# A fused attention and expert kernel: rows turned one slot sooner, and two tiles whose second layer keeps h stationary

## The chip, the cores and the metric
The kernel runs on one core of a Trainium2 chip. Its time is the device time of one launch in microseconds (us). Before the change the median of three runs is 2148.25 us (2147.32 to 2149.73).

## What is computed
The reference first computes an attention without softmax over 8 batches of 2496 tokens, and then sends each token through one of 8 experts, a layer of 1024 and a layer back to 256, by the largest logit.
```python
scores = z @ z.T / S
x = u * (np.maximum(scores, 0) ** 2 @ v)          # 8 x 2496 rows of 256
logits = x @ w_gate + modality_bias[modality_id]
e = argmax(logits); gate = softmax(logits)[e]
out[token] = gate * (np.maximum(x @ w1[e], 0) @ w2[e])
```

## The kernel before, in words
**Precision.** A value that enters a product is split into a high part, rounded by ScalarE, and a low part, the remainder that VectorE takes; a product is three products (high x high, high x low, low x high).

**The attention part** runs to about 1249 us in the profile. As it goes, each token's row is scattered by GpSimd (`scatter`, L718 to L720) to its expert's stretch of a DRAM table `xs`. Nothing that the change touches lies there.

**The expert part** takes tiles of 512 rows of one expert (`run_tile`, called by the loop near the program's end). The tiles are t = -4 to 34: four early ones of the fullest expert (EARLY = 4), whose rows are complete before the rest is routed, and 35 whole ones (UNC = 35). After tile 34's first half stands a quarter tile (`quarter_tile`, 128 rows, lines L1496 to L1521), woven into tile 34. What may remain is handled by branches at the end (L1656), which this input skips. For tile t:

- `fetch` (L875, L877) brings rows out of `xs` into `xg`, one or two tiles ahead. `turn_blocks` (VectorE, `xt`, L941), `part_high` (ScalarE, `xh`, L948) and `part_low` (VectorE, `xl`, L953) turn them and split them. They run inside the tile before, at the slot that `turn_at` gives for the transposition and one slot later for the split.
- The first layer, `up`, makes for f = 0 to 7 six products of 512 columns into `ph` (L1365); ScalarE takes `hh` from it (L1369), VectorE `hl` (L1370). f runs in two groups of four.
- The second layer follows each group. In a **staged** tile, `down` holds w2 stationary and streams h: per group sixteen products with hh and then eight with hl, of 512 columns (L1439), into two banks `po`. The result stands turned, with features on partitions. So `send` transposes it on VectorE (`squared`, L1451), stores it in a DRAM buffer `stage` by four transfers (L1455), and leaves the rest for the next tile: at its slot 2 one load `back` (L1464), at slots 4, 5, 6, 6 a scaling by the gate on ScalarE (L1469) and the put of 128 rows by GpSimd (L1389).
- In a tile that is **not staged**, `down_high` and `down_low` hold h stationary: per group sixteen products of 512 columns (L1376, both halves of w2 side by side) and sixteen of 256 columns (L1380), into four banks. Rows stand on partitions at once, and `finish` puts them out at the tile's end: per 128 rows two scalings `part` on ScalarE (L1420) and two sums `y` on VectorE (L1421), in turn, and a put on GpSimd (L1389).
- Inside a tile, `aside(f)` is called at slots f = 0 to 9. Slot 5 comes after `up` of f = 5; slot 6 after that of f = 7, ahead of the second layer; slot 7 within or after the second layer. It emits what was put off, then a quarter of the next tile's weight split (`part_weights_high`, ScalarE, L918; `part_weights_low`, VectorE, L922) at slots 2 to 5, and then the turning.

**Order.** Every engine works its instructions in the order in which this code emits them (the schedule is manual). SP carries the loads and stores, GpSimd the row transfers.

**The puts.** A tile's first put waits until the four of the tile before have landed, since two tiles of an expert may share rows. Tile 34 and the quarter tile are **kept**: their rows are put after the skipped branches, the quarter tile's first, and the others after it has landed. On the skipped path GpSimd's queue waits until earlier row transfers have landed before it goes on.

Before the change all tiles but 34 are staged:
```python
def is_staged(t):
    return t < UNC - 1
def turn_at(t):
    return {-EARLY: 3, 1 - EARLY: 3, UNC - 1: 2}.get(t, KF - 2)
```

Of the kernel before, what the change touches and what calls it, by code (L numbers as in the profile page):

```python
# [9 lines left out]
F32 = mybir.dt.float32  # L10
# [6 lines left out]
P = 128  # L17
# [10 lines left out]
def tile_attention_moe(ctx: ExitStack, tc: tile.TileContext, ut, v, zt, mid, wg, mb, w1, w2, out):  # L28
# [12 lines left out]
    B, S, D = v.shape  # L41
# [4 lines left out]
    KD, KF = D // P, F // P  # L46
    J = T // P
# [8 lines left out]
    EARLY = min(4, (B - 1) * S // E // T)  # L56
    UNC = -(-N // T) - EARLY
# [796 lines left out]
        ready["n"] = len(scatters)  # L854

    def is_staged(t):
        return t < UNC - 1

    def fetch(t, r0=0, nj=J):

        n = t + EARLY
        cell = first[0:1, 1:2] if t < 0 else meta[0:1, t, 0:1]
        row = nc.sync.value_load(cell, min_val=0, max_val=(E - 1) * CAP if t < 0 else E * CAP - T)
        k = fetched["n"] % 2
        fetched["n"] += 1
        nt = nj * P
        xg = head[k].tile([P, T // BLK, KD * BLK], F32, tag=f"xg{k}", name="xg")[:, 0:nt // BLK, :]
        side = small.tile([P, J, 2], F32, tag="gate", bufs=4, name="gate")[:, 0:nj, :]
        r0 += n * T if t < 0 else 0
        src = xs[bass.ds(row + r0 if r0 else row, nt), :]  # L870
        dmas = []
        for b in range(P // BLK):
            cols = slice(b * KD * BLK, (b + 1) * KD * BLK)
            rows_of = src[:, cols].rearrange("(t i) c -> i t c", i=BLK)
            dmas.append(nc.sync.dma_start(out=xg[b * BLK:(b + 1) * BLK], in_=rows_of))  # L875
        order = "(p j) c -> p j c" if is_staged(t) else "(j p) c -> p j c"
        dmas.append(nc.sync.dma_start(out=side, in_=src[:, D:XW].rearrange(order, j=nj)))  # L877
        wait_rows([ins_of(i) for i in dmas])
        TL[t] = (side, xg)
# [315 lines left out]
    with tc.manual_schedule(engines={ET.PE, ET.Activation, ET.DVE, ET.Pool, ET.SP}):  # L1195
# [33 lines left out]
        def ready_at(p):  # L1229
            t = 0.0  # L1230
            for d, lag in p.after:
                if d.start is None:
                    return None
                t = max(t, d.end + lag)
            return t
# [14 lines left out]
        while left:  # L1250
# [6 lines left out]
            for p in lists[e][:80]:  # L1257
                t = ready_at(p)
# [89 lines left out]
    mp = ph2.enter_context(tc.tile_pool(name="mp", bufs=2, reuse_waits="tile"))  # L1348
# [37 lines left out]
    def put_rows(ids, j, y, group):  # L1386

        i = ins_of(
            nc.gpsimd.indirect_dma_start(  # L1389
                out=out,  # L1390
                out_offset=bass.IndirectOffsetOnAxis(ap=ids[:, j:j + 1], axis=0),
                in_=y,
                in_offset=None,
                bounds_check=N - 1,
                oob_is_err=False,
            )
        )
        tc.declare_no_dep(i, group=group, reason="a tile's tokens are distinct")
        tc.add_to_no_dep_group(group, i)
        for s in done:  # L1400
            tc.add_manual_dep(i, s.name, data, reason="rows that two tiles of an expert share")
        return i

    def finish(t, po, group, kept=None):

        side, TL[t] = TL[t][0], None
        tag = "ids" if kept is None else "kept_ids"
        ids = mp.tile([P, J], I32, tag=tag, bufs=4 if kept is None else 2, name="ids")[:, 0:len(po)]
        nc.vector.tensor_copy(out=ids, in_=side[:, :, 1])
        mine = []  # L1410
        for j in range(len(po)):
            gate = side[:, j, 0:1]
            part2 = mp.tile([P, D], F32, tag="part2", bufs=2, name="part2")
            keep = kept is not None
            y = mp.tile([P, D], F32, tag="kept" if keep else "y", bufs=J + 1 if keep else 2, name="y")
            of_y = y.rearrange("p (b k c) -> p k b c", k=KD, c=BLK)
            for k in range(KD):
                cols = slice(k * P, (k + 1) * P)
                high, low = po[j][:, cols], part2[:, cols]
                nc.scalar.mul(out=low, in_=po[j][:, D + k * P:D + (k + 1) * P], mul=gate)  # L1420
                nc.vector.scalar_tensor_tensor(  # L1421
                    out=of_y[:, k], in0=high.rearrange("p (b c) -> p b c", c=BLK), scalar=gate,
                    in1=low.rearrange("p (b c) -> p b c", c=BLK), op0=ALU.mult, op1=ALU.add,
                )
            if keep:
                kept.append((ids, j, y, group))
            else:
                mine.append(put_rows(ids, j, y, group))
            if j == len(po) - 1 and not kept:
                done[:] = mine  # L1430
                written.extend(mine)
            yield
# [91 lines left out]
        yield from finish(t, [po], f"out{t}{part}", kept)  # L1524

    def turn_at(t):
        return {-EARLY: 3, 1 - EARLY: 3, UNC - 1: 2}.get(t, KF - 2)

    def run_tile(t, ahead, extra={}, part="", beside=iter(()), kept=None):
        if len(TL[t]) < 3:  # L1530
            turn(t)
        staged = is_staged(t) and not part
        po = [ps_o.tile([P, 2 * D], F32, tag="o", name="po") for _ in range(KD if staged else TL[t][0].shape[1])]
        h = {}
# [96 lines left out]
    kept = []  # L1631
# [89 lines left out]
```

## Time and profile before
| | us |
|---|---|
| median of three runs | 2148.25 |
| the profiled execution | 2147.46 |
| its span in the profile | 2145.7 |
| TensorE busy | 2115.1 (99%) |
| VectorE busy | 1617.1 (75%) |
| ScalarE busy | 1443.2 (67%) |
| GpSimd busy | 404.4 (19%) |

The span runs from the first to the last instruction; the execution's own time has 1.8 us more around it. The granted clock of TensorE is 0.996 of full speed over the span, so its time is 2.4 GHz time nearly throughout. Busy times of the engines overlap. The ends of products are modelled, so their starts are what is compared below. In time-line rows the brackets at the end tell how long the engine idled before the instruction and what released it; PEld is the weight load that runs beside the products.

### The profile page before, as it was taken

The numbers are of one execution on the slowest core, as the hardware profiler recorded it, in microseconds if no ns is written. First come the engines' busy times: TensorE is split into PE (matmuls) and PEld (weight loads), VectorE is DVE, ScalarE is ACT, GpSimd is POOL, SyncE is SP. The second block draws the span as 40 slices with busy tenths as digits, with TensorE's granted clock in tenths as the row PEclk, the third lists the DMA queues.
The fourth block names the chain that finished last, engine by engine and source line by source line (L and its number), as shares of the span: only waits on it lengthen the run. The fifth ranks groups of instructions, "written<-read, shape, count | busy, mean of one in ns | idle before, by whom it ended". The sixth has DMA issues, their size and how long they took to land.

```text
span 2145.7 us, 44124 instructions
## 1 busy us (share of the span) xinstructions
PE 2115.1 (99%) x16582; PEld 1842.8 (86%) x16582; DVE 1617.1 (75%) x2363; ACT 1443.2 (67%) x2214; POOL 404.4 (19%) x342
## 2 busy tenths in 40 slices
PE   9999999999999999999999999999999999999995
PEld 7888999888888899999999987888888888888884
DVE  8888889888889799799799765666566666656663
ACT  8778788788788788688788753454444545444453
POOL 0000210310300301301302304122222212212121
PEclk9999999999999999999999999999999999999998
DMA  7987877877976966967967826676766767676661
GB/s 193 281 238 168 254 202 180 255 202 181 274 186 164 300 176 163 300 174 183 288 160 181 255 61 191 176 207 177 192 192 186 205 175 207 179 189 196 185 196 48
DMA packets 630122, 424.83 MB, mean 198 GB/s; under 512 B 216170, under 2 KB 579690, under 8 KB 629898
## 3 DMA queue, kind: packets, MB, share of 16 engines
q1 hardware_dynamic: 614810, 380.72, 66.7%
q0 software_dynamic: 15088, 41.21, 5.4%
q8 instruction: 131, 2.15, 0.4%
q14 instruction: 93, 0.76, 0.1%
HBM read 263.66 MB, written 158.13 MB: 197 GB/s over the span
## 4 chain that ended last, share of the span: by engine, by line
PE 75%; DVE 11%; ACT 5%; DMA 4%; issue 3%; SPq 1%; POOL 0%; ACTq 0%; POOLq 0%; DVEq 0%
PE acc L492 44%; PE ph L1365 13%; PE po L1439 10%; PE s L343 6%; DVE hl L1370 3%; DVE w L922 3%; DVE xl L953 2%; DMA out_dram<-back,ids 2%; DVE xt L941 2%; ACT xh L948 2%; ACT w L918 2%; PE po L596 2%; DMA squares<-turn 1%; SPq L416 1%; ACT back L1469 1%
## 5 line engine op out<-in xcount | busy, mean ns | idle before, releaser
L492 PE MATMUL acc<-ah,vh 64*128 64x512 f32 (+1 forms) x3120 | 460.2, 384 | 0.9 <-DVE ah L439 0.5
L492 PE MATMUL acc<-al,vh 64*128 64x512 f32 (+1 forms) x3120 | 449.5, 382 | 0.1
L466 DVE TENSOR_TENSOR al<-r,ah 128x1024 fp32r<-128x1024 f32 (+4 forms) x514 | 431.6, 873 | 23.7 <-ACT ah L456 21.6
L492 PE MATMUL acc<-ah,vl 64*128 64x512 f32 (+1 forms) x3120 | 448.4, 382 | 0.0
L1369 ACT ACTIVATE hh<-ph 128x512 fp32r<-128x512 f32 x312 | 182.9, 600 | 369.1 <-PE ph L1365 369.1
L720 POOL DMA_INDIRECT xs<-x,sloti x160 | 195.2, 1220 | 1097.8 <-ACT ah L456 385.4
L1365 PE MATMUL ph<-xh,w 128*128 128x512 f32 x1248 | 399.0, 390 | 0.3 <-ACT xh L948 0.3
L1370 DVE SCALAR_TENSOR_TENSOR hl<-ph,hh 128x512 fp32r<-128x512 f32 x312 | 211.5, 688 | 249.0 <-ACT hh L1369 248.9
L456 ACT CAST ah<-r 128x1024 fp32r<-128x1024 f32 (+5 forms) x475 | 333.8, 746 | 38.5 <-PE acc L492 24.0
L492 PEld LDWEIGHTS acc<-al,vh 64*128 64x128 f32 x3120 | 332.6, 184 | 26.9 <-DVE al L466 0.8
L492 PEld LDWEIGHTS acc<-ah,vh 64*128 64x128 f32 x3120 | 327.3, 184 | 27.1 <-DVE ah L439 0.9
L492 PEld LDWEIGHTS acc<-ah,vl 64*128 64x128 f32 x3120 | 327.0, 184 | 26.4
L1389 POOL DMA_INDIRECT out_dram<-back,ids x152 | 199.8, 1314 | 623.0 <-ACT w L918 557.0
L1439 PE MATMUL po<-hh,w 128*128 128x512 f32 x1216 | 288.6, 389 | 1.1 <-ACT hh L1369 1.1
L1365 PEld LDWEIGHTS ph<-xh,w 128*128 128x128 f32 x1248 | 234.3, 188 | 49.0 <-ACT xh L948 0.7
L1439 PEld LDWEIGHTS po<-hh,w 128*128 128x128 f32 x1216 | 228.1, 188 | 49.2 <-ACT hh L1369 2.0
L356 ACT ACTIVATE r<-s 128x1024 f32<-128x1024 f32 (+2 forms) x206 | 209.3, 1017 | 84.3 <-PE s L343 67.3
L1365 PE MATMUL ph<-xl,w 128*128 128x512 f32 x624 | 246.9, 396 | 2.9 <-DVE xl L953 0.8
L398 DVE STREAM_TRANSPOSE turn<-r 128x1024 f32<-128x1024 f32 x158 | 195.6, 1238 | 33.6 <-ACT r L432 24.1
L432 ACT ACTIVATE r<-r 128x1024 f32<-128x1024 f32 (+2 forms) x205 | 215.7, 1053 | 5.4
L343 PE MATMUL s<-zm 64*128 64x512 f32 (+3 forms) x1452 | 203.8, 377 | 1.7 <-ACT r L356 1.5
L922 DVE TENSOR_TENSOR w<-wq,w 128x1024 fp32r<-128x1024 f32 x148 | 178.2, 1223 | 33.0 <-ACT w L918 32.9
(173 smaller groups left out, 1988.1 us busy)
## 6 DMA issues: line engine op xcount, KB each, us to landing
squares<-turn SPq DMA_DIRECT2D x632, 128.0 KB, 2.9
r<-squares SPq DMA_DIRECT2D x158, 512.0 KB, 5.6
wq<-in_moe_w_dram SPq DMA_DIRECT2D x148, 512.0 KB, 5.7
ut<-in_ut_dram SPq DMA_DIRECT2D x40, 512.0 KB, 3.8
xg<-xs SPq DMA_DIRECT2D x156, 128.0 KB, 3.7
stage<-squared SPq DMA_DIRECT2D x152, 128.0 KB, 2.9
back<-stage SPq DMA_DIRECT2D x38, 512.0 KB, 3.7
vr<-in_v_dram SPq DMA_DIRECT2D x32, 512.0 KB, 7.3
```

The lines of the kernel that those rows point to most:

```text
L343: nc.tensor.matmul(out=s[t][:, w], lhsT=lhs, rhs=mv[halves[t], ql, w], start=n == 0, stop=n == 2)
L356: nc.scalar.activation(out=r[:, t, w], in_=s[t][:, w] if g < 2 else s[:, :, w], func=AF.Relu, scale=INV)
L398: nc.vector.transpose(out=turned_to, in_=x)
L432: nc.scalar.square(out=a[:, t, w], in_=r[:, t, w])
L456: copy(out=y, in_=x)
L466: nc.vector.tensor_tensor(out=y, in0=x, in1=h.bitcast(F32), op=ALU.subtract)
L492: nc.tensor.matmul(out=acc[b, c][r][dh][:, :w], lhsT=V[b, k // J][y][halves[r], k % J, dh * P:(dh + 1) * P], rhs=x[halves[r], t, :w], star ...
L922: nc.vector.tensor_tensor(out=lo, in0=x, in1=hi.bitcast(F32), op=ALU.subtract)
L1365: nc.tensor.matmul(out=ph, lhsT=lhs, rhs=rhs[:, k, :], start=n == 0, stop=n == 3 * KD - 1)
L1370: nc.vector.scalar_tensor_tensor(out=hl, in0=ph, scalar=0.0, in1=hh.bitcast(F32), op0=ALU.max, op1=ALU.subtract)
L1389: nc.gpsimd.indirect_dma_start(out=out, out_offset=bass.IndirectOffsetOnAxis(ap=ids[:, j:j + 1], axis=0), in_=y, in_offset=None, bounds_ch ...
L1439: nc.tensor.matmul(out=po[k], lhsT=w[:, f, q, k * P:(k + 1) * P], rhs=h[f][part], start=f == q == part == 0, stop=f == KF - 1 and part == 1,)
```

## The change
Three lines change.
```diff
@@ -854,7 +854,7 @@
         ready["n"] = len(scatters)
 
     def is_staged(t):
-        return t < UNC - 1
+        return t < UNC - 2 and t != 2 - EARLY
 
     def fetch(t, r0=0, nj=J):
 
@@ -1412,7 +1412,7 @@
             gate = side[:, j, 0:1]
             part2 = mp.tile([P, D], F32, tag="part2", bufs=2, name="part2")
             keep = kept is not None
-            y = mp.tile([P, D], F32, tag="kept" if keep else "y", bufs=J + 1 if keep else 2, name="y")
+            y = mp.tile([P, D], F32, tag="kept" if keep else "y", bufs=J + 1 if keep else J, name="y")
             of_y = y.rearrange("p (b k c) -> p k b c", k=KD, c=BLK)
             for k in range(KD):
                 cols = slice(k * P, (k + 1) * P)
@@ -1524,7 +1524,7 @@
         yield from finish(t, [po], f"out{t}{part}", kept)
 
     def turn_at(t):
-        return {-EARLY: 3, 1 - EARLY: 3, UNC - 1: 2}.get(t, KF - 2)
+        return {-EARLY: 3, 1 - EARLY: 3, UNC - 1: 2}.get(t, KF - 3 if is_staged(t) else KF - 2)
 
     def run_tile(t, ahead, extra={}, part="", beside=iter(()), kept=None):
         if len(TL[t]) < 3:
```
`is_staged` now leaves out t = 33 (UNC - 2) and t = -2 (2 - EARLY) besides t = 34: these two run `down_high`, `down_low` and `finish`. `y` gets four buffers, one for each put of a tile. `turn_at` gives slot 5 in place of 6 for the staged tiles from -1 to 32; tiles -2 and 33 keep slot 6, and -4, -3 and 34 keep theirs.

VectorE's order in one staged tile of the many, from its last weight remainder on (`w`), with hl of f = 6 and 7, the next tile's `xt` and `xl`, and its own `squared`:
```order
 L1370 SCALAR_TENSOR_TENSOR hl<-ph,hh 128x512
 L922 TENSOR_TENSOR w_1_20158<-wq,w_1_20158 128x4x256
-L1370 SCALAR_TENSOR_TENSOR hl<-ph,hh 128x512 x2
-L941 STREAM_TRANSPOSE xt<-xg 128x1024
+L941 STREAM_TRANSPOSE xt<-xg 128x1024
+L1370 SCALAR_TENSOR_TENSOR hl<-ph,hh 128x512 x2
 L953 TENSOR_TENSOR xl<-xt,xh 128x1024
 L1451 STREAM_TRANSPOSE squared<-po 128x16x32 x2
```

The transposition stands ahead of the last two hl; the remainder `xl` keeps its place behind them. On ScalarE the order of a staged tile is the same as before.

ScalarE from the end of tile -2 (its `xh` for tile -1) to `xh` for tile 0, before:
```order
L948 CAST xh<-xt 128x1024
L1369 ACTIVATE hh<-ph 128x512 x4
L918 CAST w_1_20157<-wq 128x1024 x2
L1369 ACTIVATE hh<-ph 128x512
L1469 ACTIVATE back<-back,gate 128x256
L918 CAST w_1_20158<-wq 128x4x256
L1369 ACTIVATE hh<-ph 128x512
L1469 ACTIVATE back<-back,gate 128x256
L918 CAST w_1_20158<-wq 128x4x256
L1369 ACTIVATE hh<-ph 128x512 x2
L1469 ACTIVATE back<-back,gate 128x256 x2
L948 CAST xh<-xt 128x1024
```

and now:
```order
L948 CAST xh<-xt 128x1024
L1420 ACTIVATE part_20940<-po,gate 128x128 x2
L1420 ACTIVATE part_20953<-po,gate 128x128 x2
L1420 ACTIVATE part_20966<-po,gate 128x128 x2
L1420 ACTIVATE part_20979<-po,gate 128x128 x2
L1369 ACTIVATE hh<-ph 128x512 x4
L918 CAST w_1_20157<-wq 128x1024 x2
L1369 ACTIVATE hh<-ph 128x512
L918 CAST w_1_20158<-wq 128x4x256
L1369 ACTIVATE hh<-ph 128x512
L918 CAST w_1_20158<-wq 128x4x256
L1369 ACTIVATE hh<-ph 128x512 x2
```

The four scalings of `back` inside tile -1 are gone, and eight scalings `part` stand ahead of tile -1's first hh.

GpSimd's row transfers, from the last scatter to the branches (`back` are rows of staged tiles, `y` rows of tiles that are not):
```order
 L1389 DMA out_dram<-back,ids 19968x256
 L720 DMA xs<-x,sloti 159744x258
-L1389 DMA out_dram<-back,ids 19968x256 x147
+L1389 DMA out_dram<-back,ids 19968x256 x3
+L1389 DMA out_dram<-y,ids 19968x256 x4
+L1389 DMA out_dram<-back,ids 19968x256 x136
+L1389 DMA out_dram<-y,ids 19968x256 x4
 L1654 TENSOR_LOAD nq
 L1656 COMPARE_AND_BRANCH
```

Tile -2's and tile 33's four puts read `y` in place of `back`; the number and the order of the puts stay, and those of tile 33 are still the last ahead of the branches. From SP's queue the four stores and the load of these two tiles are gone.

## Rows read from the trace of the kernel before
**Rows 1.** The page, part 1 (busy, instructions) and part 5 (ScalarE's hh).
```profile
PE 2115.1 (99%) x16582; PEld 1842.8 (86%) x16582; DVE 1617.1 (75%) x2363; ACT 1443.2 (67%) x2214; POOL 404.4 (19%) x342
...
L1369 ACT ACTIVATE hh<-ph 128x512 fp32r<-128x512 f32 x312 | 182.9, 600 | 369.1 <-PE ph L1365 369.1
```

**Rows 2.** The first layer's line L1365: idle before it by releaser (us, times).
```profile
  DVE xl L953: 18.3, 36
```

**Rows 3.** Busy time by window: us, PE, PEld, DVE, ACT, POOL, PEclk, DMA, GB/s.
```profile
1294.76:1316.52 21.76, 21.76 (x97) 18.02 (x96) 12.07 (x33) 7.31 (x13) 12.57 (x13) 1.00 0.69 215
1341.70:2071.82 730.12, 728.09 (x3168) 592.11 (x3168) 453.68 (x562) 358.57 (x561) 177.26 (x132) 1.00 0.69 191
```

**Rows 4.** Time line (start, us, engine), the end of one tile from 1556.98.
```profile
1556.98 1.23 DVE L922 TENSOR_TENSOR w<-wq,w 128x1024 fp32r<-128x1024 f32 x1
...
1557.81 0.92 ACT L1469 ACTIVATE back<-back,gate 128x256 f32<-128x256 f32 x2
1558.12 1.28 DVE L1370 SCALAR_TENSOR_TENSOR hl<-ph,hh 128x512 fp32r<-128x512 f32 x2
1559.32 1.24 DVE L941 STREAM_TRANSPOSE xt<-xg 128x1024 f32<-128x1024 f32 x1
...
1560.59 1.05 ACT L948 CAST xh<-xt 128x1024 fp32r<-128x1024 f32 x1 [1.86 <-DVE xt L941]
1560.69 1.98 PE L1439 MATMUL po<-hl,w 128*128 128x512 f32 x8
1561.68 1.23 DVE L953 TENSOR_TENSOR xl<-xt,xh 128x1024 fp32r<-128x1024 f32 x1 [1.12 <-ACT xh L948]
...
1562.96 0.19 PEld L1365 LDWEIGHTS ph<-xl,w 128*128 128x128 f32 x1 [0.48 <-DVE xl L953]
```

**Rows 5.** Time line of tile -1's second half, TensorE and ScalarE.
```profile
1327.40 0.39 PE L1365 MATMUL ph<-xh,w 128*128 128x512 f32 x1
...
1332.43 0.51 ACT L1469 ACTIVATE back<-back,gate 128x256 f32<-128x256 f32 x1 [2.87 <-DMA back<-stage]
...
1334.42 1.19 PE L1439 MATMUL po<-hh,w 128*128 128x512 f32 x4 [0.51 <-ACT hh L1369]
...
1341.70 0.50 PE L1365 MATMUL ph<-xl,w 128*128 128x512 f32 x1 [0.76 <-DVE xl L953]
```

**Rows 6.** TensorE in tile 34, and the waits' view of line L1380's weight loads.
```profile
2093.94 0.50 PE L1365 MATMUL ph<-xl,w 128*128 128x512 f32 x1
...
2102.91 2.08 PE L1380 MATMUL po<-w,hl 128*128 128x256 f32 x16
2104.82 0.63 PE L1496 MATMUL ph<-w,xh 128*128 128x512 f32 x2
...
L1380 PEld LDWEIGHTS po<-w,hl x32: 187/188/192, 2102.7 to 2123.0; 128*128 128x128 f32 x32
```

**Rows 7.** ScalarE's first and last scaling of the last four output rows.
```profile
2119.31 0.37 ACT L1420 ACTIVATE part<-po,gate 128x128 f32<-128x128 f32 x1 [0.41 <-PE po L1380]
...
2124.36 0.37 ACT L1420 ACTIVATE part<-po,gate 128x128 f32<-128x128 f32 x1 [0.42 <-DVE y L1421]
```

**Rows 8.** Time line of the end: VectorE's y and GpSimd's row transfers.
```profile
2117.31 0.35 DVE L1421 SCALAR_TENSOR_TENSOR y<-po,gate,part 128x128 f32<-128x128 f32 x1 [0.43 <-ACT part L1420]
2120.06 0.97 POOL L1389 DMA_INDIRECT out_dram<-back,ids  x1 [0.30 <-DVE y L1421]
2124.76 0.35 DVE L1421 SCALAR_TENSOR_TENSOR y<-po,gate,part 128x128 f32<-128x128 f32 x1 [0.43 <-ACT part L1420]
2127.56 0.97 POOL L1389 DMA_INDIRECT out_dram<-y,ids  x1 [6.53 <-issue]
2131.69 0.97 POOL L1389 DMA_INDIRECT out_dram<-y,ids  x1 [3.17 <-DMA out_dram<-y,ids]
...
2135.53 0.97 POOL L1389 DMA_INDIRECT out_dram<-y,ids  x1 [0.31 <-issue]
```

**Rows 9.** The program's last line L1717, on GpSimd's queue.
```profile
L1717 POOLq DRAIN  x3: 40/113/11743, 2133.1 to 2145.4; - x3
```

## The prediction
> **What bounds the kernel now.** I read the page's busy shares first, then the waits on the line of the first layer's products, then the time line where those waits fall, and last the end of the run. TensorE is busy for 99% of the span [rows 1], so time can only come from TensorE's few pauses or from the stretch after its last product. In the expert part one pause repeats. The line of the first layer's products waited 36 times, 18.3 us in all, for `xl`, the low half of the next tile's turned rows [rows 2]. What it costs is read from two windows [rows 3]. From the start of tile -2 to the start of tile -1, a tile that begins without the pause, 21.76 us pass and TensorE is busy for all of them. From the second product of tile 0 to the second product of tile 33, 33 tiles with the pause, 730.12 us pass, 22.125 each. The pause thus costs 0.365 us a tile: less than the wait that is shown, since the second product could not have begun at once.
>
> Where it comes from stands in one such tile's end [rows 4]. VectorE finishes the last weight remainder `w` (1556.98), then hl of f = 6 and 7 (1558.12, 1.28 us for two), then turns `xt` (1559.32, 1.24 us); ScalarE rounds `xh` (1560.59) and VectorE takes `xl` (1561.68, 1.23 us). The next tile's second product begins at 1562.96, after a wait of 0.48.
>
> Two more places lose time once. In tile -1 ScalarE waits 2.87 us for the bytes of tile -2 to come back through DRAM (`back`, 1332.43); `hh` stands behind it, so TensorE waits in the second layer, and the second product of tile 0 comes at 1341.70 [rows 5]. At the end the last y is formed at 2124.76 + 0.35, but the last row transfer is issued at 2135.53 [rows 8]: GpSimd puts tile 33's rows until 2120.06 + 0.97, must see them land before it passes the skipped branches, and only then puts the kept rows.
>
> **The change, part by part.**
> *A. Turning one slot sooner (tiles -1 to 32).* No work is added: one transposition moves ahead of hl 6 and hl 7, and `xh`, `xl` ahead of the second layer's issue. By [rows 4]: `xt` would run from 1558.12 to 1559.36 and hl 6 and 7 after it until 1560.60. They are what is late next: the products that read hl begin at 1560.69 and take 0.227 each (5.44 us for 24, a quarter of 21.76), and the third needs hl 6 at 1561.14, the fourth hl 7 at 1561.37, so 0.77 us of slack are left. On ScalarE the two `back` scalings ahead of `xh` end at 1558.73, so `xh` runs from 1559.40 to 1560.45 and `xl` from about 1560.6 to 1561.85. TensorE, unbroken, wants `xl` at 1560.69 + 9 x 0.227 = 1562.73: 0.9 us to spare. The pause goes whole: 33 x 0.365 = **-12.0 us**. Its bounds are half of that, if something not shown takes the rest, and the whole, since 21.76 is TensorE's own work. The rows to be turned were fetched a tile earlier, so that the transposition sits on no transfer.
>
> *B. Tile -2 with h stationary.* It drops two transpositions of po, four stores and one load on SP's queue, and four scalings in tile -1, and adds eight ScalarE scalings and eight VectorE sums right at its end; its four puts only come sooner. The `back` wait of tile -1 has nothing left to wait for. Tile -1's second half began at 1327.40, so unbroken (10.88 us, half of 21.76) its successor's second product would come at 1327.40 + 10.88 + 0.23 = 1338.51; it came at 1341.70 [rows 5]. That is 3.2 us. In tile -1 the sooner turning applies as well. Against it stands the weight loading. In tile 34, which already works this way, sixteen products of 256 columns begin at 2102.91 and the next line at 2104.82, 1.91 us against 8 x 0.227 = 1.81 for the same columns in the other order [rows 6]. So 0.1 a group, two groups, 0.2. **B = -3.0 us** (bounds -1.5 and -3.2).
> The Trainium skill ("TensorE: Matmul & The Clock Gate", sections "LDWEIGHTS (loading the stationary operand)" and "Back-to-back issue gap") speaks against this part: it has the spacing of products set by weight load and product together, and gives a load of 128 columns as P/1.2, 107 ns. Were each of the 32 short products of a tile to carry that on top, an estimate by that page is 3.4 us a tile, 6.8 us for the two, and the sum would be about -17.7. The row of tile 34 disagrees: 0.119 us a product, loads of 188 ns beside it.
> What can hold tile -1 up is the output chain, which runs ahead of its first hh on ScalarE. In tile 34 four rows take from 2119.31 to 2124.36 + 0.37, 5.42 us, paced by TensorE there [rows 7]. TensorE needs the first hh 5.44 us after the tile starts, and the chain starts before the tile does. I cost it at nothing; uncovered it would be about one hh, 0.60 [rows 1].
>
> *C. Tile 33 with h stationary.* Its rows are ready within its own end and the first 5 us of tile 34, so GpSimd puts them some 20 us before tile 34 ends and passes the branches while that tile still runs. The first kept put then waits for its own y alone (2117.31 + 0.35), and goes out at about 2118.0 instead of 2127.56. The second waited 4.13 us for it to land (2131.69), and the others follow at 1.28 [rows 8]. So puts at 2118.0, 2122.1, 2123.4, 2124.7, 2125.95; the last y (2125.11) is in time. The last put comes 2135.53 - 2125.95 = 9.6 us sooner. The drain on GpSimd's queue after it, 11.7 us long [rows 9], I take to shift with the last put. **C = -9.6 us**, bounds -5 (the drain gives some back) and -10.1 (only the last y binds).
>
> *D. Tile 33 into tile 34.* Tile 33 still turns at the old slot, so that pause stays (`xl` at 2093.94 [rows 6]), and it hides the 0.2 us of short products. The chain of y starts behind that `xl`: four rows at 5.42 us end at 2099.4 at the latest, and the first hh (0.60) comes at 2100.0, where TensorE wants it 23 products after 2093.94, at 2099.2; unpaced by TensorE the rows go faster and nothing is late. VectorE's weight remainders shift with it, up to 1.3 us on the quarter tile. Between 0 and 1.8 I take **+0.3**, near the lower end, because in [rows 7] ScalarE and VectorE idled between rows.
>
> **Sum.** -12.0 - 3.0 - 9.6 + 0.3 = -24.3. The profiled execution took 2147.46, so 2123.2; the median of the runs is 2148.25, 0.8 above it, so **2124.0 us**.
>
> **The rivals.**
> 1. *The tail stays.* The kept rows are put late for another reason than tile 33's rows, the branches themselves, say. For it: 6.53 us ahead of the first kept put have no named releaser [rows 8]. Against: the stretch begins right where the last rows of tile 33 go out, and the kept put reads nothing later than its own y. Then -14.7: 2133.6. Chance 0.08.
> 2. *The next one late.* ScalarE's queue keeps `xh` back: it stands behind two `back` scalings, and these behind a load from DRAM that a shorter tile gives less time. From 0.9 us of lateness on the pause is back; I price it at half of A: -18.3, 2130. Against: in [rows 4] the scalings follow hh without a wait. Chance 0.12.
> 3. *The outputs at once cost more* than 0.3: hh and the quarter tile's `xl` late behind eight scalings, 1.8 in tile 34 and 0.6 in tile -1: 2126.1, and 2129 if the drain also takes part of C. Chance 0.07.
> 4. *The weight loads show.* The short products can't go faster than their loads, 188 ns each [rows 6], once VectorE and GpSimd work beside them: 32 x (0.188 - 0.119) = 2.2 a tile, 4.4 for two, 2128.4. Against: the same loads ran at 0.119 in tile 34. Chance 0.02. By the page of the Trainium skill named under B it would be 2130.6.
> 5. *Slower.* hl 6 and hl 7 become the path: the transposition ahead of them makes every second layer wait. The price is s a tile in place of 0.365. With s = 1.24, the whole transposition: 33 x (1.24 - 0.365) = +28.9, with B to D +16.6: 2164.9. It decides from 0.77 us of lateness on; s = 0.74 would eat the gain, s over 0.87 would make the kernel slower by over 0.2%. Against: the slack is read from one tile, but all 33 show the same pattern. Chance 0.04, half of it slower by that much, half within it.
> That the sooner turning is not issued sooner is excluded by the order of instructions.
>
> **The numbers.** 0.2% is 4.3 us, about what a measurement can tell from no change; the three runs shown spread over 2.4. The forecast has 0.67. A forecast with all terms at their far bounds, -12.0 - 3.2 - 10.1 = -25.3, gives 2122.9, less that spread 2120.5. Rivals 2 to 4 lie below 2131, rival 1 at 2133.6, so the range goes from 2120.5 to 2134, and leaves out rival 5 and two terms that miss together. Faster 0.96 (all but rival 5), same 0.02 and slower 0.02 (its halves).
>
> **What would show it.** Right: the waits for `xl` on the first layer's line fall from 36 to about 3; tile 0 to tile 33 takes 718 us; no wait for `hl` on the second layer's line there; in tile -1 no wait for hh; the last put follows the last y by about 1 us and the span ends some 10 us after that. Wrong: a wait for `hl` in every tile (rival 5), a put still at over 10 us behind the last y (rival 1), an hh wait at the head of tile -1 or 34 (rival 3).

## The result, and the profile after

The changed kernel takes 2122.27 us in the median of four runs (2121.24 to 2125.74), the kernel before 2148.68 beside it (four runs, 2147.32 to 2149.73). The ratio is 0.988, 95% interval 0.9863 to 0.9897, so it is faster by more than the 0.2% of the prediction; the time lies 1.7 us below the forecast of 2124.0. The span of the profiled execution falls from 2145.7 to 2119.5 us.

The page of the changed kernel, parts 1 (busy, share, instructions; the first row of [rows 1] answers to it) and 4 (the chain that ended last, by engine; before, TensorE had 75% of it, VectorE 11%, ScalarE 5%, DMA 4%):
```profile
PE 2103.9 (99%) x16614; PEld 1841.3 (87%) x16614; DVE 1622.1 (77%) x2375; ACT 1444.7 (68%) x2222; POOL 432.1 (20%) x342
...
PE 97%; DMA 1%; issue 1%; ACT 0%; POOL 0%; POOLq 0%; DVE 0%; DVEq 0%
```
The chain is TensorE's now. What ended the idle time ahead of the first layer's products (us, times; against [rows 2]):
```profile
  PE acc L492: 0.3, 1
  DVE xl L953: 0.3, 1
```
The 36 waits for `xl` have become one; the prediction had about three left. The second layer's line L1439, which waited for hh four times before (3.1 us), waits for nothing now.

Busy time by window, the same two stretches as in [rows 3] (us, PE, PEld, DVE, ACT, POOL, PEclk, DMA, GB/s):
```profile
1293.23:1316.03 22.80, 22.49 (x113) 18.68 (x112) 12.18 (x34) 7.85 (x15) 12.24 (x13) 1.00 0.70 213
1338.05:2056.13 718.08, 718.08 (x3170) 594.60 (x3168) 457.94 (x562) 358.64 (x561) 206.16 (x132) 1.00 0.70 194
```
From tile 0's to tile 33's second product 718.08 us pass where 730.12 passed, and TensorE is busy for all of them: 33 tiles of 21.76. The first row, tile -2, got longer (22.80 against 21.76); more on this below.

The end of one regular tile, the time line (start, us, engine), to be held against [rows 4]:
```profile
1549.90 1.23 DVE L922 TENSOR_TENSOR w<-wq,w 128x1024 fp32r<-128x1024 f32 x1
...
1550.72 0.92 ACT L1469 ACTIVATE back<-back,gate 128x256 f32<-128x256 f32 x2
1551.04 1.24 DVE L941 STREAM_TRANSPOSE xt<-xg 128x1024 f32<-128x1024 f32 x1
1552.20 1.25 DVE L1370 SCALAR_TENSOR_TENSOR hl<-ph,hh 128x512 fp32r<-128x512 f32 x2
...
1552.31 1.05 ACT L948 CAST xh<-xt 128x1024 fp32r<-128x1024 f32 x1 [0.67 <-DVE xt L941]
...
1553.39 1.23 DVE L953 TENSOR_TENSOR xl<-xt,xh 128x1024 fp32r<-128x1024 f32 x1
...
1553.61 1.98 PE L1439 MATMUL po<-hl,w 128*128 128x512 f32 x8
```
The transposition stands ahead of the two hl. VectorE no longer idles ahead of `xl` (before: 1.12 us), because `xh` is rounded while VectorE makes hl 6 and 7. `xl` is ready at 1554.62; the next tile's second product begins at 1555.65, 1.03 us later. Hl 7 is ready at 1553.45 and its product, the fourth of the eight, begins at 1554.29.

In tile -1 the second half runs from 1326.94 to the second product of tile 0 without a wait (TensorE's time line; against [rows 5]):
```profile
1326.94 0.39 PE L1365 MATMUL ph<-xh,w 128*128 128x512 f32 x1
...
1332.38 3.79 PE L1439 MATMUL po<-hh,w 128*128 128x512 f32 x16
1336.01 1.98 PE L1439 MATMUL po<-hl,w 128*128 128x512 f32 x8
1337.82 0.39 PE L1365 MATMUL ph<-xh,w 128*128 128x512 f32 x1
1338.05 0.39 PE L1365 MATMUL ph<-xl,w 128*128 128x512 f32 x1
```
The end, a time line of VectorE's last y and of GpSimd's row transfers, tile 33's first and last and then those of the kept tiles, against [rows 8]:
```profile
2079.57 0.97 POOL L1389 DMA_INDIRECT out_dram<-y,ids  x1 [2.68 <-DVE y L1421]
...
2083.40 0.97 POOL L1389 DMA_INDIRECT out_dram<-y,ids  x1 [0.30 <-issue]
2101.88 0.97 POOL L1389 DMA_INDIRECT out_dram<-y,ids  x1 [17.50 <-DVE y L1421]
2105.06 0.97 POOL L1389 DMA_INDIRECT out_dram<-y,ids  x1 [2.21 <-DVE y L1421]
...
2108.69 0.35 DVE L1421 SCALAR_TENSOR_TENSOR y<-po,gate,part 128x128 f32<-128x128 f32 x1 [0.44 <-ACT part L1420]
2109.32 0.97 POOL L1389 DMA_INDIRECT out_dram<-y,ids  x1 [0.42 <-issue]
```
and the program's last line on GpSimd's queue (ns min/median/max, first and last start), against [rows 9]:
```profile
L1717 POOLq DRAIN  x3: 40/113/9528, 2109.1 to 2119.2; - x3
```
Tile 33's last put goes out at 2083.40, 25 us ahead of the last y (before: 4.7 ahead). The kept puts follow their y, the last 0.63 us after the start of the last y.

What GpSimd's queue does at the skipped branches (L1656), the first line before, the second now:
```profile
L1656 POOLq INC_SWDGE_SEM  x1: 2111/2111/2111, 2124.3 to 2124.3; - x1
L1656 POOLq INC_SWDGE_SEM  x1: 2111/2111/2111, 2086.0 to 2086.0; - x1
```
Before, this step began 4.2 us after the start of tile 33's last put (2120.06), took 2.1, and the first kept put came 1.2 us behind it: together the 7.5 us from 2120.06 to 2127.56. Now it is over at 2088.1, 13.8 us ahead of the first kept put.

The two spans place by place; all products are taken at their start ("second" is a tile's second product):

| stretch | before | after | change | predicted |
|---|---|---|---|---|
| start to the first product of the expert part | 1249.25 | 1247.71 | -1.54 | 0 |
| tiles -4 and -3 | 45.51 | 45.52 | 0.0 | 0 |
| tile -2 to tile 0's second | 46.94 | 44.82 | -2.12 | B -3.0 |
| tile 0's second to tile 33's | 730.12 | 718.08 | -12.04 | A -12.0 |
| tile 33's second to tile 34's | 22.11 | 22.10 | 0.0 | D +0.3, with the next |
| tile 34's second to the last y | 30.83 | 30.47 | -0.36 | |
| last y to last put | 10.77 | 0.63 | -10.14 | C -9.6 |
| last put to the end | 10.14 | 10.15 | 0.0 | 0 |

### The profile page after: what moved, and what is told of

The parts are those of the page before. It is cut to its first block, busy times and chain, and to the rows that moved or that the text cites. A ratio compares the mean times of both kernels' runs of the same rounds, so it can differ in the third digit from the quotient of the medians.

```text
span 2119.5 us, 44183 instructions
## 1 busy us (share of the span) xinstructions
PE 2103.9 (99%) x16614; PEld 1841.3 (87%) x16614; DVE 1622.1 (77%) x2375; ACT 1444.7 (68%) x2222; POOL 432.1 (20%) x342
## 4 chain that ended last, share of the span: by engine, by line
PE 97%; DMA 1%; issue 1%; ACT 0%; POOL 0%; POOLq 0%; DVE 0%; DVEq 0%
PE acc L492 49%; PE ph L1365 19%; PE po L1439 18%; PE s L343 7%; PE po L596 2%; DMA out_dram<-back,ids 1%; PE po L1376 1%; PE po L1380 0%; PE warm L1199 0%; PE s L596 0%; ACT r L356 0%; POOL out_dram L1389 0%; DMA out_dram<-y,ids 0%; ACT r L432 0%; PE pc L684 0%
## 5 line engine op out<-in xcount | busy, mean ns | idle before, releaser
L1370 DVE SCALAR_TENSOR_TENSOR hl<-ph,hh 128x512 fp32r<-128x512 f32 x312 | 210.0, 684 | 256.4 <-ACT hh L1369 252.5
L1365 PE MATMUL ph<-xh,w 128*128 128x512 f32 x1248 | 398.3, 390 | 0.0
L1389 POOL DMA_INDIRECT out_dram<-back,ids x144 | 219.3, 1523 | 550.5 <-ACT w L918 495.3
L1365 PEld LDWEIGHTS ph<-xh,w 128*128 128x128 f32 x1248 | 234.3, 188 | 49.0 <-PE acc L492 0.3
L1439 PE MATMUL po<-hh,w 128*128 128x512 f32 x1152 | 272.8, 389 | 0.0
L1439 PEld LDWEIGHTS po<-hh,w 128*128 128x128 f32 x1152 | 216.2, 188 | 44.9
L1365 PE MATMUL ph<-xl,w 128*128 128x512 f32 x624 | 243.0, 389 | 0.0
```

The lines of the kernel that those rows point to most:

```text
L1365: nc.tensor.matmul(out=ph, lhsT=lhs, rhs=rhs[:, k, :], start=n == 0, stop=n == 3 * KD - 1)
L1370: nc.vector.scalar_tensor_tensor(out=hl, in0=ph, scalar=0.0, in1=hh.bitcast(F32), op0=ALU.max, op1=ALU.subtract)
L1389: nc.gpsimd.indirect_dma_start(out=out, out_offset=bass.IndirectOffsetOnAxis(ap=ids[:, j:j + 1], axis=0), in_=y, in_offset=None, bounds_ch ...
L1439: nc.tensor.matmul(out=po[k], lhsT=w[:, f, q, k * P:(k + 1) * P], rhs=h[f][part], start=f == q == part == 0, stop=f == KF - 1 and part == 1,)
```

## The experiments

Twelve runs were made, of nine further kernels and of the changed one again. The theory: A, B and C are independent and add up, each at its place. The rivals: A needs the other parts; the end got short for another reason than the time at which tile 33's rows are put; what tile -2 lost is a price of the short products.

**One part alone, and the changed kernel again.** These four ran on one chip, with the kernel before at 2147.82 (13 runs).

Only the turning:
```diff
-        return t < UNC - 2 and t != 2 - EARLY
+        return t < UNC - 1
```


> Only the turning is one slot sooner (staged tiles from -1 on, tile 33 among them); tiles -2 and 33 stay staged. Theory (three parts that add up, each with its own place): the pause for xl goes in tiles 1 to 34, 34 x 0.365 = 12.4 us, so about 2136.2 against 2148.6 before; the stretch from tile 0's to tile 33's second product takes 718.1 us in place of 730.1; the wait of hh in tile -1 stays, and the last put still comes 10.8 us after the start of the last y. Rival (the sooner turning needs the other parts, because the four scalings of back and the load behind them hold xh up): the stretch stays over 724 us and the time at 2141 or more. Rival (the attention part, 1.55 us shorter in the changed kernel, is made so by the change): its first product of the expert part comes at 1247.7 again and not at 1249.3.

2134.27 us, ratio 0.9936 (0.9919 to 0.9952). The stretch from tile 0 to tile 33 takes 718.08 us, the step to tile 34 21.76, the last put still comes 10.64 behind the last y: theory, and the rival that A needs the other parts falls. The wait in tile -1 stayed, as expected: from its second half to tile 0's second product it takes 13.58 us, where 11.11 is unbroken. The first product of the expert part came at 1248.73, between the two.

Only tile 33:
```diff
-        return t < UNC - 2 and t != 2 - EARLY
+        return t < UNC - 2
...
-        return {-EARLY: 3, 1 - EARLY: 3, UNC - 1: 2}.get(t, KF - 3 if is_staged(t) else KF - 2)
+        return {-EARLY: 3, 1 - EARLY: 3, UNC - 1: 2}.get(t, KF - 2)
```


> Only tile 33 keeps h stationary and puts its rows out at once; turning and tile -2 as before. Theory: the end alone gets shorter: the last put starts about 0.6 us after the start of the last y in place of 10.8, and the span ends 10.2 us after that put, as before. 10.1 us less, with the step from tile 33 to tile 34 within 0.5 of before: about 2138.4 against 2148.6; the stretch from tile 0 to tile 33 stays at 730.1. Rival (the end became short through the sooner turning, which moved everything ahead of it): the last put stays over 8 us behind the last y and the time over 2146.

2138.26, ratio 0.9957 (0.994 to 0.9974), the expected 2138.4. The stretch from tile 0 to tile 33 is 730.10. The last put comes 1.76 us behind the last y, not 0.6, and the end gave 9.0. The second kept put came 4.75 us after the first here, when its own y had been ready for 1.8 us; by the order of the code it waited for the first to land.

Only tile -2:
```diff
-        return t < UNC - 2 and t != 2 - EARLY
+        return t < UNC - 1 and t != 2 - EARLY
...
-        return {-EARLY: 3, 1 - EARLY: 3, UNC - 1: 2}.get(t, KF - 3 if is_staged(t) else KF - 2)
+        return {-EARLY: 3, 1 - EARLY: 3, UNC - 1: 2}.get(t, KF - 2)
```


> Only tile -2 keeps h stationary; turning and tile 33 as before. From the start of tile -2 to the second product of tile 0 before: 46.94 us; with all three parts 44.82. My prediction for this part was -3.0 us, the trace showed -2.12, because ScalarE took the second hh of tile -2 2.9 us late. If that pause belongs to this run only, the stretch is 43.9 to 44.3 here (the pause for xl at tile 0 stays in this kernel, 0.36) and tile -2 itself takes 21.9 us; if it comes with this way of working, the stretch is about 45.2 and tile -2 takes 22.8. The time is 2 to 3 us below before, 2145.6 to 2146.6. Rival (the weight loads of the short products show): tile -2 takes 24 us or more, without a pause of ScalarE.

2144.95, ratio 0.9986 (0.9976 to 0.9995). Tile -2 takes 22.83 us with ScalarE's pause in it; the rival of 24 us without a pause falls. I was wrong on one thing: the stretch is 44.84 and not 45.2, because no pause for `xl` is left at tile 0 (first to second product 0.23 us), though tile -1 turns at the old slot here. The scalings of `back` are gone from tile -1, and VectorE's last `w` there starts 4.87 us into the tile's second half (1333.41 after 1328.54) where it took 5.35 in the tile of [rows 4] (1556.98 after 1551.63); hl, `xt` and `xl` follow 0.5 us sooner. One scaling takes 0.51. VectorE's rows here, the last `w` and `xl`:
```profile
1333.41 1.22 DVE L922 TENSOR_TENSOR w<-wq,w 128x1024 fp32r<-128x1024 f32 x1
...
1338.10 1.23 DVE L953 TENSOR_TENSOR xl<-xt,xh 128x1024 fp32r<-128x1024 f32 x1 [1.12 <-ACT xh L948]
```
So part of the pause that A removes was ScalarE's time, passed on through VectorE's queue.

The changed kernel again:

> The changed kernel once more. Theory: 2122.3 within 2 us; from tile 0 to tile 33 718.1 us, the last put 0.6 us after the start of the last y. Open and told apart here: if the late second hh of tile -2 (ScalarE idle 3.63 us before it) and the start of the expert part at 1247.7 belong to the kernel, both are here again within 0.2 us; if they are of one run, tile -2 takes 21.9 us in place of 22.8, and the expert part begins elsewhere by 0.5 us or more.

2121.42, ratio 0.9881 (0.9865 to 0.9898). The three parts alone gave -13.55, -9.56 and -2.87, together -25.98; this run, against the same runs of before, -26.40: within the intervals (4 to 7 us wide each) they add up. ScalarE's pause in tile -2 was there again (tile -2 22.93).

**How near the next limit is.** The two runs here ran on another chip, together with the first of the sooner turning in all tiles and the first with later puts (both below), with before at 2146.62 (13 runs). The transposition twice over:
```diff
-        nc.vector.transpose(
-            out=xt.rearrange("p k (t i) -> p k t i", i=BLK), in_=xg.rearrange("p t (k c) -> p k t c", k=KD)
-        )
+        for _ in range(2 if is_staged(t - 1) and t > -1 else 1):
+            nc.vector.transpose(
+                out=xt.rearrange("p k (t i) -> p k t i", i=BLK), in_=xg.rearrange("p t (k c) -> p k t c", k=KD)
+            )
```


> The changed kernel with each transposition of the next tile's rows done twice over in tiles 0 to 32 (the same result written twice), which puts 1.16 us more of VectorE's time ahead of the rounding and of hl 6 and 7. In the changed kernel's trace hl 7 is ready 0.84 us before its first product (1553.45 against 1554.29), hl 6 1.21 us, and xl 1.03 us. Theory (the slack is as small as the profile shows, the second layer's hl is next): TensorE waits for hl 7 some 0.32 to 0.40 us a tile, 33 tiles take 10.5 to 13 us more, tile 0 to tile 33 about 730, the time about 2134. Rival (the slack is larger, since the buffers or the order let hl go ahead): the stretch stays at 718 to 720. Rival (the pause comes back whole at xl instead): waits named xl on the first layer's line, over 1 us a tile, the time over 2155.

2141.33, ratio 0.9976 (0.9967 to 0.9986); the stretch takes 738.81, 20.73 more, 0.63 us a tile and not 0.32 to 0.40. The place was right: the waits in the stretch are for hl, none for `xl`. What ended the idle time ahead of the second layer's products (us, times), and the time line of one tile (the added line moves L1439 to L1440, L1370 to L1371, L941 to L942):
```profile
  DVE hl L1371: 26.6, 67
```
```profile
1578.42 2.52 DVE L942 STREAM_TRANSPOSE xt<-xg 128x1024 f32<-128x1024 f32 x2
...
1580.77 0.41 PEld L1440 LDWEIGHTS po<-hl,w 128*128 128x128 f32 x2
1580.86 1.25 DVE L1371 SCALAR_TENSOR_TENSOR hl<-ph,hh 128x512 fp32r<-128x512 f32 x2
...
1580.99 2.60 PE L1440 MATMUL po<-hl,w 128*128 128x512 f32 x8
1581.57 0.19 PEld L1440 LDWEIGHTS po<-hl,w 128*128 128x128 f32 x1 [0.38 <-DVE hl L1371]
...
1582.16 0.99 PEld L1440 LDWEIGHTS po<-hl,w 128*128 128x128 f32 x5 [0.41 <-DVE hl L1371]
```
The wait for hl stands on the weight load (PEld), not on the product, although the load reads only w. Of 1.28 us of delay (2.52 - 1.24) 0.63 were paid, so the slack is 0.65 us. That is the 0.84 to the product's start less the 0.19 of its load: it fits a slack that is counted to the load and not to the product.

The turning two slots sooner:
```diff
-        return {-EARLY: 3, 1 - EARLY: 3, UNC - 1: 2}.get(t, KF - 3 if is_staged(t) else KF - 2)
+        return {-EARLY: 3, 1 - EARLY: 3, UNC - 1: 2}.get(t, KF - 4)
```


> The changed kernel with the turning two slots sooner than before instead of one (slot 4, the split at slot 5), in the staged tiles from -1 on. Now xl stands ahead of hl 6 and 7 on VectorE, and the rounding xh ahead of hh 6 and 7 on ScalarE. Theory (VectorE's order decides, and hl 7 is the next to be late): the work up to hl 7 grows by xl's 1.16 us against 0.84 us of slack, so TensorE waits for hl 7 about 0.3 us a tile: tile 0 to tile 33 takes 726 to 731 us, the time 2130 to 2134. Rival (sooner is simply better or the same, since nothing is late): 718 us and 2122. Rival (hh 6 becomes late behind xh on ScalarE): waits for hh on the second layer's line, over 0.5 us a tile, the time over 2138.

The edit moves the turning in tiles -2 and 33 as well, which the expectation does not say; the stretch from tile 0 to tile 33 holds staged tiles alone. 2136.13, ratio 0.995 (0.9934 to 0.9967); the stretch takes 732.90, 0.45 a tile more than in the changed kernel. My theory's size was near, its place wrong. The time line of one tile, ScalarE and TensorE:
```profile
1574.93 1.05 ACT L918 CAST w<-wq 128x1024 fp32r<-128x1024 f32 x1
...
1576.59 1.05 ACT L948 CAST xh<-xt 128x1024 fp32r<-128x1024 f32 x1 [0.61 <-DVE xt L941]
1577.55 1.08 ACT L1369 ACTIVATE hh<-ph 128x512 fp32r<-128x512 f32 x2
1578.19 1.68 PEld L1439 LDWEIGHTS po<-hh,w 128*128 128x128 f32 x8 [0.54 <-ACT hh L1369]
```
`xh` stands ahead of hh 6 on ScalarE and itself waits 0.61 for the transposition, so hh 6 is late for its products. On that line the idle time (us, times) is
```profile
  ACT hh L1369: 18.0, 33
```
That is the mechanism of the last rival in the expectation, at a smaller price. In a staged tile that also scales `back`, slot 6 is too late for `xl`, slot 4 for hh 6; slot 5 alone leaves both in time.

**The sooner turning in tiles -2 and 33 too.**
```diff
-        return {-EARLY: 3, 1 - EARLY: 3, UNC - 1: 2}.get(t, KF - 3 if is_staged(t) else KF - 2)
+        return {-EARLY: 3, 1 - EARLY: 3, UNC - 1: 2}.get(t, KF - 3)
```


> The changed kernel with the sooner turning in tiles -2 and 33 as well. In the changed kernel one wait for xl is left (0.3 us, where tile 33 passes to tile 34). Theory: the step from tile 33's to tile 34's second product falls from 22.10 to about 21.8 us and the end with it, 0.3 us in all: 2122.0 if the changed kernel is at 2122.3, which the times can't tell and the trace can. Rival (in these tiles hl 6 and 7 are needed sooner, because h is stationary and f goes through one after the other): the first layer's gain is lost on waits for hl on the line of the short products, and the step stays at 22.1 or more.

2120.05, ratio 0.9876 (0.986 to 0.9893). The last wait for `xl` is gone. The step from tile 33 to 34 falls from 22.10 to 21.99, not 21.8: the short products of tile 33, which the pause had hidden, now show (21.76 + 0.23). Tile 34 gains 0.13. On a third chip, with before at 2147.3 (7 runs), it ran beside the changed kernel:

> The changed kernel once more, beside the next one on the same chip. Theory: 0.988 of before; from the start of tile -2 to the second product of tile 0 43.8 to 44.1 us where ScalarE takes hh of tile -2 in time (as in the four runs before this), or 44.8 to 45.0 where it is late again (as in the first profile of the changed kernel and its repetition), which would say that the late hh belongs to the execution, not to the change.

> The changed kernel with the sooner turning in tiles -2 and 33 as well, once more, beside the changed kernel on the same chip. Theory: from tile 0's first product to the end of the span 0.24 us less than in the changed kernel, as in the first run of it (781.44 against 781.65); the medians 0 to 1 us apart, which the times can't tell.

2121.66 (2121.04 to 2121.72) against 2122.20 (2120.94 to 2123.39), four runs each: the times don't tell them apart. From tile 0's first product to the end of the span it takes 0.25 us less (781.39 against 781.64), 0.24 expected. In its two traces 52.31 and 52.33 us pass from tile 33's second product to the last y, against 52.55 to 52.62 in four traces of the changed kernel (the later puts of below counted among them). It is the best version seen, by an amount of which only the trace speaks.

**What made the end short.** The first attempt moved the puts of tile 33 behind slots 4 to 6 of tile 34 in the order of the code:
```diff
-                mine.append(put_rows(ids, j, y, group))
-            if j == len(po) - 1 and not kept:
+                if t == UNC - 2:
+                    put_off.append((min(4 + j, 6), lambda j=j, y=y: mine.append(put_rows(ids, j, y, group))))
+                else:
+                    mine.append(put_rows(ids, j, y, group))
...
```


> The changed kernel, but tile 33's four puts are issued at slots 4, 5, 6 and 6 of tile 34, where the puts of a staged tile stand, instead of right behind each y; the rows themselves are formed as in the changed kernel. Theory (the end got shorter because GpSimd puts tile 33's rows early and has passed the branches when the kept rows are ready): the first kept put waits again with no named releaser, the last put comes over 9 us behind the start of the last y, and the time is 9 to 10.5 us above the changed kernel, about 2131.5 to 2132.5. Rival (the end got shorter because tile 33's rows need no way through DRAM, whenever they are put): the last put stays within 2 us of the last y and the time at 2122 to 2123.

2120.32, ratio 0.9879 (0.9862 to 0.9895), the last put 0.63 behind the last y. This tells nothing on the question: GpSimd has no other work in that stretch, so a put that is written later still goes out when its y is there (the first at 2077.60, 1.69 us after tile 34's first product). It is the changed kernel once more. The second attempt, beside the changed kernel on the third chip, gave the puts something to wait for:
```diff
...
+                    def late(j=j, y=y):
+                        nc.scalar.copy(out=y, in_=y)
+                        mine.append(put_rows(ids, j, y, group))
+
+                    put_off.append((min(4 + j, 6), late))
...
```


> The changed kernel, but each of tile 33's four y is copied onto itself by ScalarE at slots 4, 5, 6 and 6 of tile 34, where a staged tile is scaled, and put behind that copy (the run before with late puts moved nothing, since GpSimd has nothing else in its queue there: its puts still went out at each y). Now the puts must wait for ScalarE. Theory (the end is short because tile 33's rows have landed before the kept rows are ready): the puts go out about 17.9 to 26.6 us after tile 34's first product, as before; the first kept put follows the last of them by 7.5 us with no named releaser, the next by 4.1, then 1.28 each; the last put comes 10 us behind the start of the last y, and the time is 9.5 to 10.6 us above the changed kernel. Rival (it is the shorter way of the rows, h stationary and no stage, that shortens the end): the last put within 2 us of the last y, the time within 1 us of the changed kernel.

2133.61, ratio 0.9931 (0.9915 to 0.9948). GpSimd's time line, tile 33's puts and the first kept ones:
```profile
2099.48 0.97 POOL L1389 DMA_INDIRECT out_dram<-y,ids  x1 [17.79 <-ACT y L1430]
...
2109.01 0.98 POOL L1389 DMA_INDIRECT out_dram<-y,ids  x1 [0.30 <-ACT part L1420]
2116.48 0.97 POOL L1389 DMA_INDIRECT out_dram<-y,ids  x1 [6.50 <-issue]
2119.80 0.97 POOL L1389 DMA_INDIRECT out_dram<-y,ids  x1 [2.34 <-DMA out_dram<-y,ids]
...
2123.63 0.98 POOL L1389 DMA_INDIRECT out_dram<-y,ids  x1 [0.30 <-issue]
```
The picture of [rows 8] is back with h stationary and no stage: the first kept put 7.47 us after tile 33's last one, 6.50 of it with no named releaser, the last put 9.54 behind the last y. The 7.47 us divide as before the change: 4.2 to the step at the skipped branches, 2.1 for it, 1.2 behind it. From tile 0's second product to the end it takes 9.5 us more than the changed kernel beside it (790.9 against 781.4); the medians differ by 11.4, and ScalarE's pause in tile -2, told below, was 2.8 us longer here.

All four copies and puts at slot 4, against the kernel just above:
```diff
-                    put_off.append((min(4 + j, 6), late))
+                    put_off.append((4, late))
...
```

> As the run with held puts, but all four copies and puts at slot 4 of tile 34, so that tile 33's last put goes out some 4 to 5 us sooner. Theory: from tile 34's first product the last of tile 33's puts comes at about +21.7 us, the first kept put 7.5 after it at +29.2 (its own y allows +24.0), the last one at +37.2 in place of +31.4: 5 to 6 us above the changed kernel, about half of the price of the run with held puts. Rival (all or nothing: one lost order of events costs the whole 10 us, wherever the last put lies): the same time as with held puts, within 1 us. Rival (nothing waits for these puts): as the changed kernel.

2127.42, ratio 0.9911 (0.9895 to 0.9928), and from tile 0's second product to the end 4.9 more than the changed kernel (5.2 by the medians):
```profile
2099.72 0.98 POOL L1389 DMA_INDIRECT out_dram<-y,ids  x1 [0.30 <-issue]
2106.23 0.97 POOL L1389 DMA_INDIRECT out_dram<-y,ids  x1 [5.54 <-issue]
2111.38 0.97 POOL L1389 DMA_INDIRECT out_dram<-y,ids  x1 [4.17 <-DVE y L1421]
...
2115.22 0.97 POOL L1389 DMA_INDIRECT out_dram<-y,ids  x1 [0.30 <-issue]
```
Tile 33's last put at +20.8 from tile 34's first product (2078.91), the first kept put 6.5 behind it, the last at +36.3, where I expected +21.7, 7.5 and +37.2. The second kept put comes 5.15 us after the first; its own y had been ready since 2107.06, so it waited for the landing again, whatever the row names. The price grows with the lateness of tile 33's last put (5.5 us later in the run before, 4.7 dearer); all or nothing falls.

## Why the prediction was right, and where its sizes were off

The forecast's case came true and rivals 1 to 5 did not. A had its size; B, C and D did not. B gave 0.9 us less than its term, C and D 0.5 and 0.7 more, so that it is in part luck that the sum, -24.67 in the spans against -24.3, is so near.

**A** was -12.0 and is -12.04, in the changed kernel and with the turning alone. The mechanism held in each row: `xt` from 1551.04, hl 6 and 7 behind it, `xl` 1.03 us ahead of need (I had 0.9).

**B** was -3.0, the profile of the changed kernel shows -2.12. The wait for `back` and the hh wait are gone as predicted, and the short products cost the predicted 0.1 a half (10.98 and 11.01 against 10.88, in the profiles without the pause told next). The missing 0.8 us is a pause of ScalarE in tile -2. ScalarE's hh of tile -2, in the changed kernel's profile:
```profile
1294.79 0.60 ACT L1369 ACTIVATE hh<-ph 128x512 fp32r<-128x512 f32 x1 [5.35 <-PE ph L1365]
1299.01 0.60 ACT L1369 ACTIVATE hh<-ph 128x512 fp32r<-128x512 f32 x1 [3.63 <-PE ph L1365]
1300.52 1.09 ACT L1369 ACTIVATE hh<-ph 128x512 fp32r<-128x512 f32 x2 [0.90 <-remote]
```
and in the run with the puts written later, which is the same there:
```profile
1293.63 0.60 ACT L1369 ACTIVATE hh<-ph 128x512 fp32r<-128x512 f32 x1 [5.35 <-PE ph L1365]
1294.99 0.60 ACT L1369 ACTIVATE hh<-ph 128x512 fp32r<-128x512 f32 x1 [0.76 <-PE ph L1365]
...
1297.71 0.60 ACT L1369 ACTIVATE hh<-ph 128x512 fp32r<-128x512 f32 x1 [0.76 <-PE ph L1365]
```
Without the pause the stretch from tile -2 to tile 0 takes 44.00, B = -2.94. The pause does not belong to the change: two kernels that keep tile -2 staged show it as well (first half of tile -2 14.71 us with the turning alone, 11.82 with tile 33 alone), and one and the same kernel, with the sooner turning in all tiles, shows 10.98 in one profile and 11.76 in the other. With the pause on both sides B is the same: 47.84 us in the kernel with tile 33 alone, 44.82 in the changed one.
The estimate that the prediction worked out from the load time of the Trainium skill ("TensorE: Matmul & The Clock Gate", "LDWEIGHTS (loading the stationary operand)"), 6.8 us for the two tiles if each short product carried its load on top, did not come. The traces show 0.23 a tile, with loads of 187 to 192 ns beside short products 0.12 us apart. Putting the load on top of each product was the prediction's own step; the section gives the load's time alone.

**C** was -9.6 and is -10.14, its outer bound. The step that failed is "the second waited 4.13 us for it to land": in the changed kernel the second kept put comes 3.18 us after the first and is released by its y, so the landing was over by then. Only the last y binds. That holds in all eight profiles with both the sooner turning and early puts of tile 33 (3.18 or 3.19 us); in the other six the second put came 3.3 to 5.2 us after the first, and why the landing took longer there stays open. The rest stood: tile 33's rows are put 25 us ahead, the drain shifts along. That the time of those puts is the cause is shown by the two runs that held them (9.5 and 4.9 us back), so rival 1 falls by experiment. It had a part of the truth: of the 7.5 us before the change 3.3 went by at the branches themselves, from the start of the step at L1656 on. They cost nothing now because they are over early.

**D** was +0.3 and is -0.37 (0.0 and -0.36). The row chain that I priced at up to 1.36 us a row ran at 1.05: its scalings waited for the y ahead of them, none for TensorE (the last y of tile 33 starts at 2082.08, the first hh of tile 34 at 2081.95). The gain lies in tile 34: four scalings of `back` left ScalarE there. With the four copies at the old slots it took 31.07 against 30.46 beside it.

**The sum.** A to D come to -24.67 in the spans. The other -1.54 lies in the attention part, where nothing changed; the same kernel began its expert part at 1247.71, 1247.87 and 1249.26 in three profiles, so a difference of this size stands between executions of one kernel. The medians fell by 26.4, 26.4 and 25.1 us in the three comparisons with before, and with the turning alone by 13.55 where its trace places 12.6. The profiles, only one of which is of the kernel before, do not settle where the last 0.4 to 1.7 us of the medians' fall lie.

**Rival 5**, the one on the slow side, had the right next limit and nearly the right distance: I put the slack at 0.77, the run with two transpositions shows 0.65. The rival lacked 0.65 us of VectorE's time a tile to come true. Rival 2 was alive too in a way: ScalarE's queue is what makes slot 4 lose.

## What to carry to other kernels

Where a repeated pause ends on one engine's last step, look for a step ahead of it that can change places with one that has slack; then read the slack of the work that was pushed back (here it fitted when counted to the weight load and not to the product), and of what stands behind every instruction that moves on the other engines. One slot too far cost 0.45 us a tile here.
Work at a program's end that must be seen to land is put as early as its data allow: what counts is the last such transfer ahead of the wait. Between the two runs that held it, 5.5 us sooner won 4.7, and once it was early enough the last y was what bound.
To delay an instruction in an experiment, give it something to wait for; writing it later on a queue that is otherwise idle moves nothing.

## What the runs showed of the hardware that I had not expected

ScalarE's hh in tile -2 came late in 9 of 14 profiles, whatever the kernel: the first half of that tile took 10.88 or 10.98 us in five profiles (before, and the four taken on one chip), 11.76 to 11.93 in seven and 14.60 or 14.71 in two. Of that, 0.1 is the short products where the tile is not staged. All eight profiles taken on two other chips show the late hh. In the changed kernel's profile hh started some 2.9 us after the products that it reads are shown as done, and the row behind it names "remote" as releaser, a semaphore update that the profile cannot place. GpSimd's scatters of the routed rows run in the same stretch, in the profiles without the pause as well. Whether it comes from them, from the profiling or from elsewhere was not tried and stays open.

From the last put to the end of the span 10.14 or 10.15 us passed in all 14 profiles, while the drain on GpSimd's queue was shown with 9.5 to 11.8 us. The length of the drain's row says nothing on its own; the last put does.

The same 132 puts kept GpSimd busy for 206 us instead of 177 in the stretch of 33 tiles: the fourth put of a tile now runs beside `xl` and takes 1.92 us in place of 0.97 (the first two run beside `w`, at 1.87 and 1.53). Of the 132, the 34 that run beside neither take 0.97, the others 1.53 to 1.92. No row shows anything waiting for it.
